# Score blocks of 32 keys by 96 queries on 64x32 array tiles, with an int32 band mask, in a fused sliding-window attention and expert-attention kernel

## The chip, the cores and the metric

The kernel runs on one core of one Trainium2 chip. The core has five engines that run from queues of their own and wait for each other with semaphores: TensorE (PE in the profile, its weight loads are PEld), VectorE (DVE), ScalarE (ACT), GpSimd (POOL) and SyncE (SP), which issues most of the DMAs. The metric is the device time in microseconds of one execution; the lower the better. The runs of the kernel before took 235.07, 235.68 and 236.68 us, with a median of 235.68 us.

## The reference, cut to what matters

Two stages follow each other. The first is attention in a sliding window of 32 keys to either side, over 8 batches, 8 heads, 576 positions and 64 dimensions. The second takes the result as `x` (8 x 576 x 512) and runs four experts, each a causal attention with one head of 64 dimensions, of which two are chosen per token by a gate.

```python
# stage 1
scores = scale * np.matmul(q, k.transpose(0, 1, 3, 2))
mask = np.abs(pos[:, None] - pos[None, :]) <= 32
scores = np.where(mask, scores, -1e9)
attn = softmax(scores); attn_out = attn @ v          # per head
# stage 2
logits = x @ w_gate                                   # two best of four experts
for e in range(E):
    q = x @ wq[e]; k = x @ wk[e]; v = x @ wv[e]
    ye = causal_softmax(scale * q @ k.T) @ v @ wo[e]
    out += weight_of(e) * ye
```

Only the band of the first stage's scores matters: key `k` counts for queries `k - 32` to `k + 32`. A block of 32 keys that starts at `32 n` is therefore needed for the 96 queries from `32 n - 32` to `32 n + 64`, and a block of 64 keys for 128 queries.

## The kernel before, in words

All of the work is cut into small steps, and `ORDER` (lines 29 to 101) lists them by hand in one long order: a name, digits for batch, head group and part, a letter for the engine, and after `@` the PSUM banks. The loop at the end (lines 745 to 755) issues the steps in this order, so each engine's queue holds its own share of the list. SP's loads are tied to their place: a load waits for the matmul that was issued last before it (`load`, line 196). Work of several batches is interleaved: the second stage of one batch stands between the first-stage steps of the next.

The steps that this document speaks of:

- `lq`, `lk`, `lv` load q, k and v. `tq` and `tk` (DVE, a transpose by blocks of 32, line 318) bring q and k to `T` with the head dimension on partitions; 32 partitions hold half a head. For batches 2 to 7 `qc` and `kc` (copies on POOL or ACT) and `mv` (four DMAs from SP, line 367) rearrange `T` so that a whole head of 64 dimensions stands on 64 partitions; this is called paired. Batch 0 gets the paired form by matmuls (`hq`, `hk`), batch 1 stays unpaired and uses matmuls with 32 rows.
- `sc` (line 389) computes the scores of one half of the queries (288 of 576) for four heads of a group, transposed: keys on the partitions, queries along the bank. Four banks hold four heads. The partition of a key is its number modulo 128, so a bank holds in each column the keys of a band about that query. A block has 64 keys, and its place `par` (partitions 0 to 63 or 64 to 127) alternates; `BLK` gives its range of queries and `SEQ` the order of the blocks. In the paired form each block is one matmul per head; the two values of `p` are the two row groups of 64 partitions, `dh` picks one of the two heads there. All 288 columns of all 128 partitions get written. Batch 0 (`NBS`) adds the mask as a matmul of -1e30 (`NB`, built by `s_nb` on DVE at line 222 from `MASKP`).
- `ex` (line 418) takes the exponential of two banks on ACT, into the float32 tile `A`.
- `mk` (line 421) multiplies `A` in place by the 0/1 band mask on POOL, for batches 1 to 7: 56 instructions of 128 x 576 elements. The mask `MASKP` is built once by POOL (`s_mask`, line 204).
- `av` multiplies `A` with the values on PE (float32, in tiles of 128x64 and 128x32); `un` normalises on DVE; `xt`, `xf`, `xb` transpose the result and cast it for the second stage.
- `pp`, `pe`, `pv`, `ve`, `ps`, `xe`, `se`, `po`, `oe`, `pt`, `ot`, `py`, `ye`, `st` and the gate steps `ga` to `gu` are the second stage, in bf16 but for the gate. `ps` with chunk 3 and some others use 64x64 array tiles.

Most matmuls and transposes are issued through the helpers at lines 191 and 194, so the profile gives these lines, and the tiles tell the steps apart: `PS<-T` is `sc`, `PS<-V,A` is `av`, `PS<-QKE` is `ps`, `PS<-XTF,WG` is `ga`, `PS<-ident,XN` is `xt`. A float32 matmul appears as two matmul rows with a weight load each.

## Time and profile before

| | before |
|---|---|
| median of three runs | 235.68 us |
| profiled execution: its time / its span | 234.73 us / 233.0 us |
| PE busy | 216.2 us (93%) |
| DVE / ACT / POOL busy | 168.2 / 161.3 / 158.9 us |
| matmul rows of `sc` (`PS<-T`) | 1440, 41.1 us busy |
| band mask on POOL (line 423) | 56 x 1412 ns, 78.2 us |

The profile is of one execution. Busy time of an engine is the time in which at least one of its instructions ran; matmuls are pipelined and their ends are modelled, so a row's length is not its cost, and the distance between the starts of successive rows says more. "Idle before, and what released it" is the time that an engine stood still just before an instruction of a group. The granted clock is a share of TensorE's full speed; its mean over the span is 0.98.

### The profile page before, as it was taken

To read this page: it belongs to the slowest core of one execution; us is meant where nothing else is said; L and a number is where in the kernel's file an instruction comes from. 1 tells how busy PE (TensorE), PEld (TensorE's weight loads), DVE (VectorE), ACT (ScalarE), POOL (GpSimd) and SP (SyncE) were. 2 spreads that over 40 slices of the span, in tenths; PEclk is the share of its full clock that TensorE was granted. 3 is DMA by queue.
4 is the path that set the end of the run, shared out by engine and by line. 5 is a ranking of instruction groups with operands and counts; after the bars stand their busy time and mean duration, and the time that the engine had idled before them with its cause. 6 is when DMAs were issued, how large, how long until landed. Compare 5 with 4: busy or idle time off the path is not lost. (4 is left out here: it accounts for less than half of the span.)

```text
span 233.0 us, 11640 instructions
## 1 busy us (share of the span) xinstructions
PE 216.2 (93%) x5089; PEld 174.4 (75%) x5100; DVE 168.2 (72%) x328; ACT 161.3 (69%) x246; POOL 158.9 (68%) x205
## 2 busy tenths in 40 slices
PE   7959959999999999999999999999999999999981
PEld 3948846778787887879778888877887778786750
DVE  1744896596899797986898699867864766748760
ACT  2225257888679868778898787758837858678742
POOL 7007037698699997996988998999909982831400
PEclk9999986999999999999999999999999999999998
DMA  6977995889899998988988789946526205051355
GB/s 217 288 202 205 267 348 128 230 222 254 234 259 242 252 303 263 278 190 230 331 252 198 190 254 286 272 150 153 122 53 183 93 3 199 9 207 59 147 205 203
DMA packets 57107, 47.69 MB, mean 205 GB/s; under 512 B 40416, under 2 KB 42976, under 8 KB 57056
## 3 DMA queue, kind: packets, MB, share of 16 engines
q1 hardware_dynamic: 56480, 45.76, 69.3%
q10 hardware_dynamic: 576, 1.18, 1.4%
q8 instruction: 40, 0.66, 1.3%
q14 instruction: 11, 0.09, 0.1%
HBM read 30.42 MB, written 9.44 MB: 171 GB/s over the span
## 5 line engine op out<-in xcount | busy, mean ns | idle before, releaser
L423 POOL TENSOR_TENSOR A<-A,MASKP 128x576 f32<-128x576 f32 x56 | 78.2, 1412 | 5.7 <-ACT A L419 5.4
L619 ACT ACTIVATE ATE<-PS 128x1024 bf16<-128x1024 f32 x48 | 47.9, 1026 | 6.0 <-PE PS L191 5.8
L624 POOL TENSOR_SCALAR_AFFINE_SELECT ATE<-ATE 128x256 bf16<-128x256 bf16 (+1 forms) x80 | 29.0, 382 | 28.7 <-ACT ATE L619 20.3
L419 ACT ACTIVATE A<-PS 128x576 f32<-128x576 f32 x64 | 38.0, 652 | 14.2 <-PE PS L191 12.9
L191 PE MATMUL PS<-T 64*64 64x128 f32 (+7 forms) x1440 | 41.1, 275 | 2.6 <-issue 2.2
L191 PE MATMUL PS<-V,A 128*64 128x65 f32 (+1 forms) x1280 | 39.4, 222 | 0.6 <-DMA V<-in_v_dram 0.5
L191 PEld LDWEIGHTS PS<-V,A 128*64 128x64 f32 (+1 forms) x1280 | 36.4, 132 | 4.6 <-issue 1.5
L191 PEld LDWEIGHTS PS<-T 64*64 64x64 f32 (+1 forms) x1440 | 34.8, 139 | 5.9 <-issue 2.8
L318 DVE STREAM_TRANSPOSE T<-qn 128x1152 f32<-128x1152 f32 x14 | 32.7, 2333 | 7.2 <-PE PS L191 5.2
L318 DVE STREAM_TRANSPOSE T<-kn 128x1152 f32<-128x1152 f32 x14 | 32.7, 2334 | 6.3 <-PE PS L191 5.6
L185 POOL COPY V<-V 64x2048 f32<-64x2048 f32 (+1 forms) x13 | 22.0, 1696 | 14.1 <-DMA V<-in_v_dram 13.8
L452 DVE TENSOR_TENSOR XN<-PS,RC 128x512 f32<-128x512 f32 x32 | 22.1, 691 | 1.2
L185 POOL CAST XTB<-XTF 128x1024 bf16<-128x1024 f32 (+1 forms) x24 | 15.4, 663 | 8.0 <-ACT XTF L183 5.0
L183 ACT COPY Y<-PS 128x1024 f32<-128x1024 f32 (+1 forms) x19 | 15.8, 849 | 5.2 <-PE PS L191 3.1
L183 ACT CAST QKE<-PS 128x576 bf16<-128x576 f32 x22 | 13.9, 644 | 7.5 <-PE PS L191 7.4
L191 PE MATMUL PS<-WO,OTT 128*128 128x512 bf16 (+2 forms) x99 | 17.9, 347 | 1.2 <-ACT OTT L183 0.5
L191 PE MATMUL PS<-WV,XTB 128*128 128x256 bf16 (+1 forms) x192 | 18.6, 256 | 0.0
L183 ACT COPY XTF<-PS 128x1024 f32<-128x1024 f32 (+1 forms) x16 | 13.6, 855 | 7.3 <-PE PS L194 5.6
L191 PE MATMUL PS<-XTB,WQ 128*64 128x288 bf16 (+1 forms) x176 | 18.6, 289 | 0.0
L191 PE MATMUL PS<-QKE 64*64 64x64 bf16 (+9 forms) x256 | 18.3, 279 | 0.1
L191 PEld LDWEIGHTS <-ATE 128*128 128x128 bf16 x480 | 16.3, 97 | 2.7 <-issue 0.9
L191 PE MATMUL PS<-XTB,WK 128*64 128x288 bf16 (+1 forms) x176 | 18.2, 286 | 0.0
(85 smaller groups left out, 301.5 us busy)
## 6 DMA issues: line engine op xcount, KB each, us to landing
V<-in_v_dram SPq DMA_DIRECT2D x32, 256.0 KB, 4.7
out_dram<-Y SPq DMA_DIRECT2D x16, 512.0 KB, 4.6
kn<-in_k_dram SPq DMA_DIRECT2D x28, 288.0 KB, 5.0
qn<-in_q_dram SPq DMA_DIRECT2D x28, 288.0 KB, 5.3
T<-T SPq DMA_DIRECT2D x48, 144.0 KB, 4.1
V<-in_v_dram SPq DMA_DIRECT2D x8, 128.0 KB, 5.1
out_dram<-Y SPq DMA_DIRECT2D x16, 64.0 KB, 3.0
qn<-in_q_dram SPq DMA_DIRECT2D x2, 320.0 KB, 4.4
```

The source lines that it names most:

```text
L183: nc.scalar.copy(o, i)
L185: eng(c).tensor_copy(o, i)
L191: last_pe[0] = nc.tensor.matmul(*a, **kw)
L318: nc.vector.transpose(T.rearrange("q h (p o) -> q h o p", o=18)[:, :, o0:o1, :], x[:, :, o0:o1, :])
L419: nc.scalar.activation(AT[(2 * b + g) % NAT_][half][p], two(b0)[:, :, 0:HS], EXP, scale=scale_att)
L423: eng(c).tensor_tensor(out=ap, in0=ap, in1=MASK[:, None, HS * half:HS * half + HS].to_broadcast([128, 2, HS]), op=MULT)
L452: nc.vector.tensor_tensor(out=XN[T // 2][:, T % 2, :].rearrange("p (t h d) -> p h t d", t=4, h=8), in0=u[:, :, 0:64].rearrange("p h (d t) ...
L619: nc.scalar.activation(chunk(A, ch), two(b0), EXP, scale=scale_moe)
L624: nc.gpsimd.affine_select(ap, ap, pattern=[[0, n], [1, w]], compare_op=IS_GE, fill=0.0, base=0, channel_multiplier=-1)
```

## The change

The scores of batches 2 to 7 are cut into blocks of 32 keys. The partition group of block `n` is `32 * (n % 4)`, as before a key's number modulo 128, and the block gets only the queries of its band within the half, at most 96. `blocks32` lists the blocks of a half for both values of `dh` in an order that gives the next block to the column group with the fewest columns so far. Each matmul names its place in the array (64 rows by 32 columns). Of each 128 columns a group of 32 partitions now gets 96 written; the other 32 keep what earlier steps left in the bank. `ex` reads the same range as before. The mask tile becomes int32, and `mk` multiplies the bits of `A` as integers by 0 or 1. Batches 0 and 1 keep their score matmuls; batch 1 uses the new `mk`. `ORDER`, banks and all other steps are unchanged.

```diff
-    MASKP = sb.tile([128, SP_], F32, name="MASKP")
+    MASKP = sb.tile([128, SP_], I32, name="MASKP")
...
-        nc.gpsimd.memset(MASKP, 1.0)
+        nc.gpsimd.memset(MASKP, 1)
...
-        nc.gpsimd.memset(MASKP[64:128, 0:64], 0.0)
-        nc.gpsimd.memset(MASKP[64:128, 576:640], 0.0)
+        nc.gpsimd.memset(MASKP[64:128, 0:64], 0)
+        nc.gpsimd.memset(MASKP[64:128, 576:640], 0)
...
+    def blocks32(half):
+        c0 = HS * half
+        todo = [[], [], [], []]
+        for n in range(S // 32):
+            lo, hi = max(c0, 32 * n - 32), min(c0 + HS, 32 * n + 64)
+            if lo < hi:
+                todo[n % 4] += [(n, lo, hi, 0), (n, lo, hi, 1)]
+        at, seq = [0] * 4, []
+        while any(todo):
+            col = min((i for i in range(4) if todo[i]), key=lambda i: at[i])
+            seq.append(todo[col].pop(0))
+            at[col] += seq[-1][2] - seq[-1][1]
+        return seq
+
+    SEQ32 = [blocks32(0), blocks32(1)]
+
     def sc(c, b, g, half, b0, b1):
         bank = (b0, b0 + 1, b1, b1 + 1)
         c0 = HS * half
 
         add = b in NBS
+        if PAIRED[g] and not add:
+            for n, lo, hi, dh in SEQ32[half]:
+                o = 32 * (n % 4)
+                for p in range(2):
+                    r = slice(64 * p, 64 * p + 64)
+                    mm(PS[o:o + 32, bank[2 * p + dh], lo - c0:hi - c0],
+                       QKT[g][r, 2 * dh, 1, 32 * n:32 * n + 32], QKT[g][r, 2 * dh, 0, lo:hi],
+                       start=True, stop=True, skip_group_check=True, tile_position=(64 * p, o))
+            return
...
     def mk(c, b, g, half, p):
-        ap = AT[(2 * b + g) % NAT_][half][p]
+        ap = AT[(2 * b + g) % NAT_][half][p][:, :, :].bitcast(I32)
         eng(c).tensor_tensor(out=ap, in0=ap,
                              in1=MASK[:, None, HS * half:HS * half + HS].to_broadcast([128, 2, HS]), op=MULT)
```

More of the change, by code (lines that the diff above doesn't have):

```diff
@@ L10 @@
 BF16 = mybir.dt.bfloat16
+I32 = mybir.dt.int32
 EXP = mybir.ActivationFunctionType.Exp
```

## The prediction

> **What bounds the kernel now.** I read the page first (busy shares), then the waits, then busy time by stretch, then the order of instructions in time on TensorE and GpSimd.

> ```profile
> span 233.0 us, 11640 instructions
> PE 216.2 (93%) x5089; PEld 174.4 (75%) x5100; DVE 168.2 (72%) x328; ACT 161.3 (69%) x246; POOL 158.9 (68%) x205
> ```
> ```profile
> ACT A L419 <- PE PS L191: 12.9, 15, 2.7
> DVE T L318 <- PE PS L191: 10.8, 6, 2.9
> PE PS L191 <- DMA V<-in_v_dram: 0.5, 1, 0.5
> ```
> ```profile
> 50.00:70.00 20.00, 19.31 (x476) 16.30 (x474) 16.82 (x27) 15.64 (x24) 17.06 (x24) 1.00 0.90 243
> 70.00:90.00 20.00, 19.70 (x515) 16.33 (x510) 16.77 (x30) 16.57 (x25) 18.38 (x23) 1.00 0.93 262
> 90.00:110.00 20.00, 19.43 (x507) 16.07 (x504) 16.61 (x28) 16.00 (x28) 17.67 (x19) 1.00 0.92 247
> 110.00:130.00 20.00, 19.89 (x485) 16.54 (x484) 16.88 (x27) 16.37 (x27) 18.11 (x20) 1.00 0.89 246
> 130.00:150.00 20.00, 20.00 (x456) 16.54 (x449) 17.70 (x32) 16.89 (x26) 19.19 (x22) 1.00 0.89 248
> ```

> From 50 us on TensorE (PE) is busy 19.3 to 20.0 of every 20 us. A busy PE is not proof, because its ends are modelled; the waits decide it. The other engines wait for PE over and over (ACT 12.9 us before the exponentials, DVE 10.8 us before the transposes), and PE's own waits are tenths of a microsecond, the longest of this kind 0.5 us for a V load. So PE sets the pace. It does not do so by much: the columns of the last view are PE, weight loads, DVE, ACT, POOL, then clock, DMA share and GB/s, and POOL (GpSimd) adds up to 90.4 of the 100 us from 50 to 150, the DMA engines are 0.89 to 0.93 busy. What PE gains can be spent only until one of these is full.

> **The change, part 1: the score matmuls.** It touches `sc` of batches 2 to 7: 6 batches x 2 head groups x 2 halves = 24 steps. Each float32 matmul stands as two in the trace. Rows from TensorE in order of time (start, length, shape of the array tile, count):

> ```profile
> 12.21 1.21 PE L191 MATMUL PS<-T 64*64 64x64 f32 x40
> 13.21 0.46 PE L191 MATMUL PS<-OTT,ident_bf 64*64 64x288 bf16 x8
> ...
> 41.31 1.36 PE L191 MATMUL PS<-T 32*64 32x64 f32 x80
> 42.60 1.29 PE L191 MATMUL PS<-XTF,WG 128*32 128x160 f32 x32
> ...
> 93.23 2.29 PE L191 MATMUL PS<-T 64*64 64x64 f32 x80
> 95.45 1.29 PE L191 MATMUL PS<-XTF,WG 128*32 128x160 f32 x32
> ```
> ```profile
> 118.25 1.29 PE L191 MATMUL PS<-XTF,WG 128*32 128x160 f32 x32
> 119.48 0.70 PE L191 MATMUL PS<-QKE 64*128 64x320 bf16 x8
> ...
> 173.56 1.28 PE L191 MATMUL PS<-T 64*64 64x64 f32 x40
> 174.78 1.55 PE L194 MATMUL PS<-ident,XN 64*64 64x64 f32 x40
> ```

> Now: a step has 20 matmuls (40 rows) on four 64x64 tiles. Its widths per parity are 96+128+64 and 160+128, 288 columns, for two head halves `dh`: 576 columns per tile. The step at 12.21 is followed by matmuls of its own tile shape after 1.00 us; the one at 173.56 by another kind after 1.22. So 1.00 us is the streaming, 1.74 ns a column, and 0.22 us the emptying of the array that a change of shape costs. Two steps in a row (93.23 to 95.45) take 2.22 = 2 x 1.00 + 0.22, which fits.

> After: blocks of 32 keys on eight 64x32 tiles (2 row groups, 4 column groups). A half has ten blocks, with `dh` and the row group 40 matmuls (80 rows): twice the instructions. Columns: 64, seven of 96, 64 and 32. The busiest column group holds 64+96+64 = 224 (or 96+96+32), with two `dh` 448 columns, in place of 576.

> Does a column cost the same there? No row shows 64x32 tiles. Two neighbours bound it. Four column tiles of 128x32 (118.25): 16 matmuls of 160 columns, 640 per tile, in 1.23 us; less the 0.22 that is 1.58 ns a column. Eight tiles of 32x64 (41.31 to 42.60): 576 per tile in 1.29, less 0.22, 1.86 ns. So 448 columns take 0.71 to 0.83 us. I take 0.80, toward the row with eight tiles: 0.20 us less per step, **24 x 0.20 = 4.8 us** (4.1 to 7.0). With twice the matmuls on fewer columns this hangs on the instruction rate: 80 rows in 0.80 us is one in 10 ns. The 32x64 step runs one in 13 ns (1.07/80) while bound by its columns, so 10 is just beyond what is shown.

> [...]

> Lost covers: where a score step stood beside another 64x64 step, the array did not have to empty; with 64x32 it must.

> ```profile
> 113.16 2.52 PE L191 MATMUL PS<-T 64*64 64x64 f32 x80
> 115.43 0.47 PE L191 MATMUL PS<-QKE 64*64 64x448 bf16 x8
> ...
> 160.43 0.43 PE L191 MATMUL PS<-QKE 64*64 64x512 bf16 x4
> ```

> Reading down TensorE's order I count six such borders from 50.98 to 160.43 (two of them around 113.16), each worth 0 to 0.22 us. I take 0.15: **0.9 us back**. Net on PE 3.9 us (2.8 to 7.0).

> **Part 2: the int32 mask.** The blocks cover the band exactly, 96 of every 128 query columns for a group of 32 keys, so the rest of the bank holds what earlier steps left. The exponential reads it (same shape as before) and the multiply by an integer 0 must clear it, whatever its bits. The 56 multiplies on POOL go from float32 to int32, same bytes, same two inputs.

> ```profile
> L423 POOL TENSOR_TENSOR A<-A,MASKP 128x576 f32<-128x576 f32 x56 | 78.2, 1412 | 5.7 <-ACT A L419 5.4
> L185 POOL COPY T<-T 128x576 f32<-128x576 f32 x14 | 9.2, 661 | 2.4 <-DVE T L318 1.9
> L222 DVE TENSOR_SCALAR OTT<-MASKP 64x640 bf16<-64x640 f32 x4 | 1.9, 486 | 0.0
> ```

> No row has POOL at an integer operation. From below: it moves as many elements as the copy with one input, 661 ns; from above I allow twice the float32 multiply, 2.8 us. The nearest row is the float32 multiply itself, 1412 ns, and I take that: **0 us**. [...]

> The mask itself is built once by POOL at the start; after it POOL stands idle 12.77 us until 18.28, so int32 fills there cost nothing. `s_nb` on DVE reads it four times at 486 ns from 7.39, with 0.54 us free behind it; were each twice as long, the first scores would start 1.4 us later. I take 0.

> ```profile
> 18.28 3.42 POOL L185 COPY V<-V 64x1536 f32<-64x1536 f32 x2 [12.77 <-DMA V<-in_v_dram]
> ```
> ```profile
> 7.39 1.98 DVE L222 TENSOR_SCALAR OTT<-MASKP 64x640 bf16<-64x640 f32 x4
> 9.91 0.82 DVE L185 COPY T<-PS 128x640 f32<-128x640 f32 x1 [0.54 <-PE PS L191]
> ```

> **What of the 3.9 us reaches the end.** Order and waits on ACT, DVE, POOL and SP stay as they are; PE alone gets shorter, and loads follow it, since SP's loads are tied to places in PE's list. Where a score step is late because its moved quarters (`mv`, SP) land late, a shorter step gains little:

> ```profile
> 148.40 2.54 SPq L367 DMA_DIRECT2D T<-T  x4
> ```
> ```profile
> 151.22 1.96 PE L191 MATMUL PS<-T 64*64 64x64 f32 x64
> 153.42 0.76 PE L191 MATMUL PS<-T 64*64 64x160 f32 x16 [0.24 <-issue]
> ```

> The fourth of these transfers is issued just before 151, and the pair from 151.22 needs 2.9 us in place of 2.2. That pair's 0.4 us I write off, and 0.1 for smaller cases of the kind. Is POOL in time? Its latest products for the value matmuls:

> ```profile
> 174.88 1.96 POOL L624 TENSOR_SCALAR_AFFINE_SELECT ATE<-ATE 128x256 bf16<-128x256 bf16 x5 [5.43 <-ACT ATE L619]
> ...
> 187.40 4.14 POOL L423 TENSOR_TENSOR A<-A,MASKP 128x576 f32<-128x576 f32 x3
> ```
> ```profile
> 190.02 1.15 PE L191 MATMUL PS<-V,A 128*64 128x65 f32 x32
> ```

> The first of the three multiplies ends near 188.8 and its user starts at 190.02: 1.2 us of slack, with PE then over 3 us ahead of today. But POOL stood idle 5.4 us at 174.88 waiting for ACT, which waits for PE, so it moves forward too. The sum is 4.8 - 0.9 - 0.5 = **3.4 us**. The profiled execution took 234.73 us (span 233.0 and 1.7 around it), which gives a span of 229.6 and 231.3 us. The median of the runs is 235.68, 0.95 above that execution, so the forecast for a median is **232.3 us**, 1.4% faster.

> **Rivals.**
> 1. *Absorbed (no change, 234 to 237).* PE's gain turns into PE's waits. For it: from 50 to 150 POOL must fit 90.4 us and the DMA engines about 90 into 97, with the order fixed for the old lengths. Against it: the waits point from everyone to PE, and POOL's own idle time is mostly for ACT behind PE. If two thirds go, 1.1 us stay: 234.6.
> 2. *The int32 multiply is slower (slower than before).* Place: POOL, 40 multiplies from 50 to 150.

> ```profile
> 50.00:70.00 20.00, 7.93 (x6) 1.00 0.90 243
> 70.00:90.00 20.00, 11.78 (x9) 1.00 0.93 262
> 90.00:110.00 20.00, 10.81 (x9) 1.00 0.92 247
> 110.00:130.00 20.00, 9.05 (x7) 1.00 0.89 246
> 130.00:150.00 20.00, 11.43 (x9) 1.00 0.89 248
> ```

>    With d more for each, POOL holds 90.4 + 40 d. That passes PE's 96.6 at d = 0.155 us (11%), and the old 100 at 0.24 us (17%); from there the kernel is slower. At half as much again (0.71) it is 118.8: 19 us more, 254. At twice, 56 us more in this stretch less the 9.6 free, 47: 282 and over. [...]
> 3. *The matmuls do not pack (slower).* If each of the 80 rows keeps the spacing of the 64x64 pair, 2.22/80 = 27.8 ns, a pair takes 4.4 us and 12 pairs cost 26.6 us more: 262. [...] Against it: the 13 ns at 41.31.

> **Chances and range.** Forecast 0.52; absorbed 0.20; slow integer multiply 0.22, of which 0.01 so little that nothing shows; no packing 0.06. So faster by over 1% 0.52, within 1% (about what a measurement of this kernel can tell from no change) 0.21, slower 0.27. The forecast's own range is 229.3 to 233.3: net 2.8 to 7.0 us on PE, less the 0.5. The range of eight in ten goes to 246, a multiply about a third slower (40 x 0.47 = 18.8, less 9.6 free, is 9 us over), and leaves out the dearer multiplies (0.13), the matmuls that don't pack and a little below.

> **What would show it.** PE's rows `PS<-T` become 64*32, about 2400 in place of 1440; two steps in a row last 1.8 us (1.6 to 1.9) in place of 2.2: right for part 1; 4.4 would be rival 3. The group L423, then int32, should read near 1412 ns; above 1570 POOL binds, with waits of PE on POOL and no more idle time of POOL on ACT. If both are as I say and the span stays, the waits of PE on DMA, DVE or ACT must have grown, and rival 1 holds. What would make me wrong beyond these: a clock granted at less than 1.00 after 50 us, or the exponential taking longer on what the banks hold outside the band.

## The result

The changed kernel is slower. Its runs took 263.25, 263.48, 265.22 and 271.65 us, median 264.35, and a fifth 267.16, beside 235.07 to 237.18, median 236.18, for the kernel before on the same chip. The profiled execution is the one of 271.65 us, a slow one, which the ratio leaves out: the ratio of the means of the others to before is 1.121, with a 95% interval of 1.110 to 1.132. The forecast was 232.3 us and its range ended at 246.0. A second profile of the same kernel (268.51 us, below under `after_again`) stops at every instruction at which this one stops for long.

First the page of the changed kernel: span and busy times, the granted clock in 40 slices, the queue that brings instructions, the shares of the chain that ended last, and two of the costliest groups. New lines shift the numbers: the helper at 191 is now 192, and the instructions of `ex` and `mk` have the lines 447 and 452.

```profile
span 269.9 us, 13560 instructions
...
PE 228.1 (84%) x6049; PEld 179.8 (67%) x6060; DVE 168.9 (63%) x328; ACT 161.8 (60%) x246; POOL 159.0 (59%) x205
...
PEclk9988998999996799799959997999799899999998
...
q8 instruction: 47, 0.77, 1.2%
...
PE 72%; issue 12%; ACT 5%; POOL 3%; DVE 3%; DMA 3%; SPq 1%; ACTq 0%; DVEq 0%
...
L452 POOL TENSOR_TENSOR A<-A,MASKP 128x576 int32<-128x576 int32 x56 | 78.1, 1409 | 8.3 <-ACT A L447 8.1
...
L192 PE MATMUL PS<-T 64*32 64x96 f32 (+9 forms) x2400 | 39.8, 249 | 20.3 <-issue 19.7
```

DVE, ACT and POOL have the busy times of before, within 0.7 us. PE's rose by 11.9 us, in an execution with far more half clock than before (5 in the row PEclk; the experiments come back to it), but its share fell from 93% to 84%: it stands idle for 41.8 us of the span, in place of 16.8. The chain says what kind of idle time this is: 12% of the span, some 32 us, is "issue", time in which PE waited for nothing that the profile shows. The last group carries 19.7 us of that kind ahead of the score matmuls. The int32 multiply takes 1409 ns, as the float32 one did (1412).

The waits of the changed kernel (engine, line, waited for: total us, times, longest):

```profile
POOL ATE L653 <- ACT ATE L648: 37.6, 11, 5.4
ACT A L447 <- PE PS L192: 28.8, 20, 3.7
PEld PS L192 <- issue: 28.5, 29, 4.0
PE PS L192 <- issue: 26.4, 14, 3.9
```

And of the kernel before, the row of the same kind, which the prediction left out:

```profile
PE PS L191 <- issue: 2.2, 2, 1.9
```

From 2.2 us in 2 waits to 26.4 us in 14. ACT and POOL still wait for PE, directly or by way of ACT, for longer than before. By stretch, in the order of columns used in the prediction:

```profile
50.00:70.00 20.00, 16.52 (x544) 13.29 (x547) 14.39 (x28) 12.46 (x19) 14.80 (x23) 1.00 0.80 212
70.00:90.00 20.00, 16.13 (x430) 13.24 (x420) 13.02 (x15) 14.14 (x23) 15.17 (x18) 0.84 0.79 210
90.00:110.00 20.00, 15.15 (x565) 12.37 (x564) 13.34 (x21) 11.97 (x18) 14.59 (x15) 0.99 0.64 197
110.00:130.00 20.00, 18.23 (x503) 15.04 (x502) 13.26 (x25) 12.76 (x21) 12.15 (x14) 0.91 0.73 199
130.00:150.00 20.00, 16.15 (x410) 11.83 (x404) 12.47 (x21) 11.84 (x20) 13.01 (x14) 0.83 0.56 161
```

PE is busy 82.2 of these 100 us (98.3 before), and the mean clock of four stretches is below 1.00 (0.83 to 0.99). The DMA engines have room now: 0.56 to 0.80 busy, where they were at 0.89 to 0.93.

Where PE stands still is seen in its order in time (start, length, row group, idle before in brackets):

```profile
51.86 2.29 PE L192 MATMUL PS<-T 64*32 64x64 f32 x160
54.08 0.41 PE L192 MATMUL PS<-QKE 64*64 64x320 bf16 x8
54.51 1.27 PE L192 MATMUL PS<-V,A 128*64 128x65 f32 x36
58.12 1.04 PE L192 MATMUL PS<-V,A 128*64 128x65 f32 x28 [2.33 <-issue]
...
78.70 2.06 PE L192 MATMUL PS<-T 64*32 64x32 f32 x160 [0.21 <-ACT VE L184]
80.68 0.62 PE L192 MATMUL PS<-WO,OTT 128*64 128x512 bf16 x4
84.97 1.06 PE L192 MATMUL PS<-WO,OTT 128*64 128x512 bf16 x4 [3.66 <-issue]
...
104.77 2.10 PE L192 MATMUL PS<-T 64*32 64x32 f32 x151
110.77 0.32 PE L192 MATMUL PS<-T 64*32 64x64 f32 x9 [3.90 <-issue]
```

Two things stand here. A pair of score steps that nothing disturbs takes 1.98 us (78.70 to 80.68): shorter than the 2.22 of before, not as short as the 1.80 forecast. And just behind such a pair, or nine rows from the end of one, PE stops for 2 to 4 us in the middle of a row of like matmuls: between the 36th and the 37th of one `av`, between the fourth and the fifth of one `po`, between the 151st and the 152nd row of one score pair. The profile shows no late tile there: the idle time is "issue", and the next matmul belongs to the same step as the last.

Counting PE's instructions (matmuls, weight loads and some 60 waits for semaphores) up to each stop gives the place. A stop is measured here from the start of the last instruction ahead of it to the next start, so it holds the 0.2 to 0.4 us of that last matmul too and is a little longer than the idle time in the rows above. All twelve stops of more than 0.8 us between 40 and 215 us come at the same point of a block of 256:

```
changed kernel: stop at us, its length, instructions recorded before it, (that number + 67) mod 256
 55.6 2.56  2751   2  |  68.6 0.83  3263   2  |  80.9 4.04  4031   2
 98.5 1.85  4798   1  | 106.6 4.12  5309   0  | 125.0 1.20  6077   0
132.4 3.64  6589   0  | 156.0 0.94  7613   0  | 159.2 2.99  7869   0
181.3 1.65  8893   0  | 189.8 2.55  9404 255  | 210.5 2.26 10428 255
```

The 67 is the shift that fits all of them; the count is of records, of which a few can be missing, hence 2 at the start and 255 at the end. The instruction queue's row tells of the same unit: 47 packets with 0.77 MB are 16.4 KB each, and the changed kernel has 12,172 recorded instructions on PE, 47.5 blocks of 256; the kernel before has 40 packets and 10,252 instructions, 40.0 blocks. Such a packet starts after PE enters a block (0.4 to 3.2 us after, from 50 to 215 us of this execution), and what it brings is needed at the end of that block. A changed pair is 160 matmul rows with as many weight loads, 320 instructions in 2 us, more than a whole block. **The theory that was tested: PE used up its instructions faster than blocks of them came in, and stood still until the next block was there.** The rivals were that the new tile shape or the unwritten banks slow PE down, that the int32 multiply does, and that only the data transfers hold the blocks up.

### The profile page after: what moved, and what is told of

Its sections match the earlier page's. It is cut to its first block, busy times and chain, and to the rows that moved or that the text cites. A ratio compares the mean times of both kernels' runs of the same rounds, so it can differ in the third digit from the quotient of the medians.

```text
span 269.9 us, 13560 instructions
## 1 busy us (share of the span) xinstructions
PE 228.1 (84%) x6049; PEld 179.8 (67%) x6060; DVE 168.9 (63%) x328; ACT 161.8 (60%) x246; POOL 159.0 (59%) x205
## 4 chain that ended last, share of the span: by engine, by line
PE 72%; issue 12%; ACT 5%; POOL 3%; DVE 3%; DMA 3%; SPq 1%; ACTq 0%; DVEq 0%
PE PS L192 65%; PE PS L195 5%; POOL A L452 3%; PE PS L239 2%; DMA V<-in_v_dram 2%; DVE T L319 1%; ACT XTF L184 1%; DMA T<-T 1%; SPq L198 1%; ACT A L447 1%; ACT ATE L648 1%; ACT V L184 1%; DVE XTF L186 0%; POOL XTB L186 0%; ACT VE L184 0%
## 5 line engine op out<-in xcount | busy, mean ns | idle before, releaser
L452 POOL TENSOR_TENSOR A<-A,MASKP 128x576 int32<-128x576 int32 x56 | 78.1, 1409 | 8.3 <-ACT A L447 8.1
L447 ACT ACTIVATE A<-PS 128x576 f32<-128x576 f32 x64 | 38.2, 651 | 32.2 <-PE PS L192 28.8
L192 PE MATMUL PS<-T 64*32 64x96 f32 (+9 forms) x2400 | 39.8, 249 | 20.3 <-issue 19.7
L192 PEld LDWEIGHTS PS<-T 64*32 64x32 f32 (+2 forms) x2400 | 33.8, 113 | 25.6 <-issue 22.4
L192 PE MATMUL PS<-V,A 128*64 128x65 f32 (+1 forms) x1280 | 40.7, 227 | 2.5 <-issue 2.3
L192 PEld LDWEIGHTS PS<-V,A 128*64 128x64 f32 (+1 forms) x1280 | 37.8, 136 | 6.9 <-issue 4.6
L186 POOL COPY V<-V 64x2048 f32<-64x2048 f32 (+1 forms) x13 | 22.0, 1693 | 13.3 <-DMA V<-in_v_dram 12.9
L192 PE MATMUL PS<-WO,OTT 128*128 128x512 bf16 (+2 forms) x99 | 18.8, 363 | 4.7 <-issue 3.7
L192 PE MATMUL PS<-XTB,WQ 128*64 128x288 bf16 (+1 forms) x176 | 20.2, 304 | 1.8 <-POOL A L452 1.0
L192 PE MATMUL PS<-WV,XTB 128*128 128x256 bf16 (+1 forms) x192 | 20.6, 272 | 0.7 <-issue 0.7
L192 PE MATMUL PS<-XTB,WK 128*64 128x288 bf16 (+1 forms) x176 | 20.9, 307 | 0.0
L192 PEld LDWEIGHTS <-ATE 128*128 128x128 bf16 x480 | 17.6, 102 | 2.6 <-issue 1.1
L192 PE MATMUL PS<-VE,ATE 128*128 128x65 bf16 x480 | 19.0, 200 | 0.0
```

The lines of the kernel that those rows point to most:

```text
L186: eng(c).tensor_copy(o, i)
L192: last_pe[0] = nc.tensor.matmul(*a, **kw)
L447: nc.scalar.activation(AT[(2 * b + g) % NAT_][half][p], two(b0)[:, :, 0:HS], EXP, scale=scale_att)
L452: eng(c).tensor_tensor(out=ap, in0=ap, in1=MASK[:, None, HS * half:HS * half + HS].to_broadcast([128, 2, HS]), op=MULT)
```

## The experiments

Each was compared with the kernel before on the same chip. "Stops" are those of over 0.45 us at the end of a block of 256 instructions that begin between 50 and 215 us of the span, measured as above; the kernel before has two, with 1.0 us.

### The int32 mask alone

```diff
-    MASKP = sb.tile([128, SP_], F32, name="MASKP")
+    MASKP = sb.tile([128, SP_], I32, name="MASKP")
...
-        ap = AT[(2 * b + g) % NAT_][half][p]
+        ap = AT[(2 * b + g) % NAT_][half][p][:, :, :].bitcast(I32)
```

> The kernel before with the int32 mask and the int32 multiply alone; scores as before. Theory A (TensorE's instructions arrive in blocks of 256, and 160 rows per score step use them up faster than the next block comes): 234 to 238 us, the multiply at 1.41 us. Theory B (64x32 tiles stall inside the array): the same. Theory C (the integer multiply or its data cost the time): 250 us or more.

Measured: 236.32 us beside 235.97, a ratio of 1.003 (0.998 to 1.008): no difference. The group of the multiply, on its page:

```profile
L424 POOL TENSOR_TENSOR A<-A,MASKP 128x576 int32<-128x576 int32 x56 | 78.3, 1414 | 5.8 <-ACT A L420 5.4
```

1414 ns for int32, 1412 for float32. The mask is out of it; the score blocks make the loss.

### The new tiles with few instructions

The changed kernel with each 64x32 tile given one matmul of 288 columns per head half: 32 rows per step on the same eight tiles, in place of 80.

```diff
-                todo[n % 4] += [(n, lo, hi, 0), (n, lo, hi, 1)]
+                todo[n % 4].append((n, lo, hi))
+        for i in range(4):
+            n = todo[i][0][0]
+            todo[i] = [(n, c0, c0 + HS, 0), (n, c0, c0 + HS, 1)]
```

> The kernel after, with the score steps of batches 2 to 7 still on eight 64x32 tiles, but one matmul per tile and head half, 288 columns wide: 16 matmuls (32 rows) per step in place of 40 (80). It leaves out the right scores (each group of 32 partitions uses the keys of its first block alone). Columns per tile: 576, as on 64x64 tiles before. Theory A: no idle time of TensorE on issue of a microsecond or more from 50 us on, two steps in a row in 2.1 to 2.3 us, 233 to 238 us in all. Theory B: steps of 2.5 us and more, 250 us or more.

Measured: 233.86 us beside 235.97, a ratio of 0.995 (0.991 to 0.9996). A pair in time, and PE's wait:

```profile
72.65 2.18 PE L192 MATMUL PS<-T 64*32 64x288 f32 x64 [0.21 <-ACT VE L184]
74.76 1.05 PE L192 MATMUL PS<-WO,OTT 128*64 128x512 bf16 x8
```
```profile
PE PS L192 <- issue: 1.6, 3, 0.8
```

The long stops are gone (1.6 us in all), with the tile shape and the int32 multiply still there. So the shape isn't what costs. This kernel also writes every column of the banks; that unwritten parts don't cost either is shown by the next one, which stops with all columns written. The pair is 2.11 us for 576 columns per tile and step; less the 0.12 to 0.22 that the rows show where another tile shape follows (`e7_half_dose` and the kernel before), that is 1.64 to 1.73 ns a column, within the 1.58 to 1.86 that the prediction took from its two neighbours.

### More instructions on the old tiles

The kernel before, each score matmul of batches 2 to 7 cut in two by columns: 80 rows per step as in the changed kernel, 64x64 tiles, float32 mask.

```diff
+                mid = (lo + hi) // 2
+                for lo_, hi_ in (((lo, hi),) if add else ((lo, mid), (mid, hi))):
-                for p in range(2):
+                    for p in range(2):
```

> The kernel before (float32 mask, 64x64 tiles), each score matmul of batches 2 to 7 cut in two halves by columns: 40 matmuls (80 rows) per step, the same columns. Theory A: TensorE idle on issue for 15 to 30 us, in pieces of 1 to 4 us, 255 to 268 us in all. Theory B: 235 to 240 us.

Measured: 263.8 us (261.78 and 265.82) beside 235.97. Its order in time and its wait:

```profile
78.11 3.02 PE L191 MATMUL PS<-T 64*64 64x32 f32 x160 [0.21 <-ACT VE L183]
81.06 0.62 PE L191 MATMUL PS<-WO,OTT 128*64 128x512 bf16 x4
84.71 1.06 PE L191 MATMUL PS<-WO,OTT 128*64 128x512 bf16 x4 [3.03 <-issue]
```
```profile
PE PS L191 <- issue: 17.9, 16, 3.1
```

The stop behind the pair at 78 is there again, after the same matmul of the same step, without new tiles, without int32 and without unwritten columns. The number of instructions alone makes the stops: 19.7 us of them, and the nine over 0.8 us between 40 and 215 us all stand at one point of a block of 256 again (instructions 2753, 3009, 4033, 4801, 5313, 6081, 6593, 7873 and 9409; remainder 4 with the shift used above). The pair itself takes 2.95 us in place of 2.22, with twice the rows for the same columns on the same four tiles (18.4 ns a row). The 24 steps, eleven pairs and two alone, count as 12 pairs: 12 x 0.73 = 8.8 us. With 18.7 us more of stops the sum is 27.5, and the span rose by 27.1 (260.1 against 233.0).

### The same columns in three pieces

The kernel with 288 columns per tile, each matmul cut into three of 96: 96 rows per step, more than the changed kernel has.

```diff
-            todo[i] = [(n, c0, c0 + HS, 0), (n, c0, c0 + HS, 1)]
+            todo[i] = [(n, c0 + 96 * j, c0 + 96 * j + 96, dh) for j in range(3) for dh in range(2)]
```

> As the wide blocks, but each 288 columns cut in three of 96: 48 matmuls (96 rows) per step on 64x32 tiles, still 576 columns per tile, scores again not the right ones. Theory A: 384 instructions per pair of steps, TensorE idle on issue 25 to 45 us, 262 to 282 us in all. On the side, in a step without such a stop: if a row cannot be issued faster than about 11 ns, the 96 rows last 1.05 to 1.1 us from first to last start; if the columns bind as in the wide blocks (0.80 us from first to last start for 288-wide matmuls), 0.9 to 1.0.

Measured: 271.86 us (268.72 and 275.0) beside 236.43.

```profile
79.97 2.46 PE L192 MATMUL PS<-T 64*32 64x96 f32 x192 [0.21 <-ACT VE L184]
82.36 1.05 PE L192 MATMUL PS<-WO,OTT 128*64 128x512 bf16 x8
```
```profile
PE PS L192 <- issue: 24.8, 16, 3.6
```

From 233.86 to 271.86 us by cutting alone: same tiles, same columns, same data. (The wait is just under the 25 us expected; the time lies within.) The undisturbed pair also tells the rate: 192 rows in 2.39 us and 160 in 1.98 are both 12.4 ns a row, and within one step from the first row to the last it is 1.119 us for 96 rows and 0.91 for 80, 11.7 and 11.4 ns. On these tiles it is the rows that set the step, not the columns.

### Half the dose

The changed kernel with the new blocks in the first half of the queries alone: 240 instructions per pair in place of 320 (160 before).

```diff
-        if PAIRED[g] and not add:
+        if PAIRED[g] and not add and half == 0:
```

> The kernel after with blocks of 32 keys in the score steps of the first half of the queries alone; the second half on 64x64 tiles as before: 240 instructions per pair of steps. Theory A with a threshold at blocks of 256: fewer and shorter stops, 240 to 250 us. Proportional to the number of changed steps: about 250.

Measured: 242.05 us (240.18 and 243.93) beside 236.43.

```profile
PE PS L192 <- issue: 9.3, 11, 2.5
```

Half of the added instructions bring 10 stops with 10.4 us, and the two runs are 3.8 and 7.5 us above the median of before: an eighth and a quarter of the 28 us, not a half. The loss depends on how fast one block is used against how fast the next comes, not on the sum of instructions.

### Lighter transfers

Two kernels ask why a block comes late. The first is the changed kernel without the loads of q, k and v from batch 3 on (the lines below stand in the two functions that load); the second has them in `mv` too and leaves out its transfers. Both compute on old data.

```diff
+        if b >= 3:
+            return
```

> The kernel after without the loads of q, k and v from batch 3 on (the tiles keep older data). Theory A, if the blocks of instructions wait behind data transfers: idle on issue falls from 26 us to 10 to 16, 243 to 254 us in all. Theory A with a delay that does not depend on the load: 258 to 266 us. Theory B: 258 to 266 us.

> The changed kernel without the loads of q, k and v and without the transfers of mv from batch 3 on, so that from there the DMA engines carry the blocks of instructions and the outputs alone. If the blocks are late because they queue behind data, a block is usable within 3 us of being asked for, idle on issue falls below 10 us and the time to 238 to 246. If most of the delay is fixed (a block's own transfer of 1 us and what follows it), it stays near 4 us, idle on issue 13 to 16 us, 246 to 250 us as with the loads alone left out.

Measured: 248.64 us beside 235.97 without the loads, 246.55 (244.57 and 248.52) beside 234.41 without the moves as well. The stretch from 50 to 150 us and PE's wait, first of the one and then of the other:

```profile
50.00:150.00 100.00, 87.76 (x2878) 71.79 (x2875) 74.06 (x117) 71.97 (x112) 81.33 (x96) 0.98 0.31 77
```
```profile
PE PS L192 <- issue: 15.5, 14, 2.0
```
```profile
50.00:150.00 100.00, 90.22 (x2924) 74.72 (x2922) 77.03 (x122) 74.91 (x116) 82.55 (x97) 0.98 0.17 48
```
```profile
PE PS L192 <- issue: 12.7, 12, 1.9
```

The DMA engines' share falls from 0.71 to 0.31 and 0.17, the rate from 196 to 77 and 48 GB/s. The stops get shorter and don't go: 17.1 and 14.1 us are left of 29.4 to 29.8. So other transfers explain two fifths to a half of what PE waits, and the rest stays with nearly empty engines. For the second kernel the expectation of a mostly fixed delay is the nearer one: 12.7 us of wait, not under 10, and a block usable after 3.6 us, not within 3 (table below).

### Batch 1 in the paired form

The kernel before has a stop of this kind too, in the one pair of steps that already had 160 matmul rows, batch 1's scores on 32x64 tiles:

```profile
30.90 0.82 PE L191 MATMUL PS<-T 32*64 32x64 f32 x40
33.66 3.60 PE L191 MATMUL PS<-T 32*64 32x96 f32 x120 [1.94 <-issue]
```

The test rearranged batch 1 too, which halves the instructions of those steps.

```diff
-    ... ex0010@0 hk010@6
+    ... ex0010@0 kc10:a hk010@6
-    ... ex0110@4 av04@4
+    ... ex0110@4 qc10:a mv10 av04@4
-    ... ex1011@2 wm1@7
+    ... ex1011@2 kc11:a qc11:a mv11 wm1@7
```

> The kernel before with batch 1 paired too (kc, qc and mv for both groups of batch 1): its four score steps take 80 instructions each in place of 160. Theory A: the stop on issue of about 2 us near 32 us goes; 232 to 235 us if nothing else holds that stretch. If TensorE waits for the weights and the first x of the second stage there anyway: 235 to 237 us.

A miss: 243.84 us beside 236.43, a ratio of 1.033 (1.023 to 1.042).

```profile
36.29 5.46 PE L191 MATMUL PS<-T 64*64 64x64 f32 x80 [3.36 <-DMA T<-T]
```

The stop for instructions is gone from this place and a wait of 3.36 us for the moved quarters is there instead, with a longer step behind it. It says nothing against the theory and is no way to a faster kernel as it was placed.

### The changed kernel again

> The changed kernel itself once more, for a profile beside the others on one chip: 260 to 267 us, TensorE idle on issue 22 to 28 us.

Measured: 268.51 and 269.72 us beside 234.41, a ratio of 1.149 (1.137 to 1.161). The time is 2 us above what was expected; PE's wait lies within.

```profile
PE PS L192 <- issue: 27.5, 18, 4.4
```

It stops at the same instructions (2751, 3263, 4031, 4798, 5309, 6077, 6589, 7613, 7869, 8893, 9404 and 10428, and two more at 2495 and 6333). What comes behind a stop in the clock can be read around the one that ends at 84.6 us (columns as before):

```profile
81.00:84.40 3.40, 0.19 (x2) 0.00 (x0) 2.03 (x1) 1.09 (x3) 3.40 (x7) 1.00 1.09 258
84.40:87.80 3.40, 3.22 (x48) 2.51 (x47) 0.28 (x2) 1.19 (x2) 1.19 (x2) 0.50 0.76 180
87.80:91.20 3.40, 3.40 (x121) 2.94 (x113) 3.35 (x4) 3.19 (x7) 0.95 (x3) 1.00 0.39 145
```

PE does next to nothing for 3.4 us, then gets half the clock for 3.4 us (48 matmuls), then the full one (121). Without the last 4 us of each span, this execution has 23.9 us at half clock, the first profile of the changed kernel 34.1, the kernel before 6.8.

### All runs by one sum

```
                      blocks  packet     stops     usable after entry  fastest use
                      (n)     ends after n, us     us, median (range)  of a block
before                30      2.5        2,  1.0   4.4 (4.1-4.7)       3.6
int32 mask alone      30      2.1        2,  1.7   5.3 (5.0-5.7)       3.6
batch 1 paired        29      2.1        1,  0.9   7.6                 3.9
new tiles, few instr. 28      2.4        2,  1.8   4.9 (4.9-5.0)       3.9
half dose             32      2.6       10, 10.4   4.6 (3.8-5.3)       2.6
old tiles, cut        33      2.6       13, 19.7   4.2 (3.3-7.6)       2.2
changed               32      2.6       14, 29.8   4.7 (3.4-5.9)       1.5
changed, again        32      2.5       14, 29.4   4.5 (3.6-6.2)       1.5
three by 96           35      2.4       18, 31.5   4.2 (3.3-5.8)       1.5
changed, no loads     35      2.3       12, 17.1   3.8 (2.6-4.5)       1.5
 and no moves         36      2.1        9, 14.1   3.6 (2.7-5.2)       1.5
```

Counted from the traces, 50 to 215 us: the blocks; the median time from entering a block (its first instruction starts) to the end of the packet that brings the next; the stops; the time from entering a block until PE went on with the next, where it had stopped; and the shortest time in which a block was used, without the stop behind it. Packets and blocks can be paired one to one, and in all 97 stops PE went on 1.1 to 1.8 us after the recorded end of the packet that brought the block it went on with. This ties the end of a stop to the packet, and not only its place to the count. In the median a block is there 3.6 to 5.3 us after the one ahead of it is entered (7.6 at the one stop with batch 1 paired). The kernel before never uses one in less than 3.6 us and hardly stops; the kernels that use one in 1.5 to 2.6 us stop nine to eighteen times.

| span less that of before (233.0) | measured | stops, less 1.0 | 12 x change of a pair | half of the added time at half clock | sum |
|---|---|---|---|---|---|
| changed | 36.9 | 28.8 | -2.9 | 13.7 | 39.6 |
| changed, again | 33.8 | 28.3 | -2.9 | 8.5 | 33.9 |
| old tiles, cut | 27.1 | 18.7 | 8.8 | 0 | 27.5 |
| three by 96 | 34.0 | 30.5 | 2.0 | 3.4 | 35.9 |
| half dose | 9.2 | 9.4 | 0.8 | -1.7 | 8.5 |

The clock's term is an upper bound, since not all of that time hung on PE. With it the stops, the pairs and the clock account for the spans to within 3 us.

## Why the prediction was wrong

**Part 1, the gain per step: mis-sized.** "24 x 0.20 = 4.8 us" came from columns: 448 at 1.58 to 1.86 ns. The column's price was right (1.64 to 1.73 in the run with few instructions), but it isn't what ends the step. The prediction said that "this hangs on the instruction rate: 80 rows in 0.80 us is one in 10 ns", and took 10 as just beyond what was shown. The tiles give one row in 11.4 to 11.7 ns, so the step takes 0.91 us and a pair 1.98: 0.12 us less per step, 2.9 us in all, where no stop falls into it.

**Part 1, what is missing: the supply of instructions.** "Order and waits on ACT, DVE, POOL and SP stay as they are; PE alone gets shorter" holds no term for it. The phrase "twice the instructions" was there, but they were counted as rows through the array and not as bytes that must be brought in (16.4 KB for 256 of them). This step failed, and it is the whole loss: 28 to 29 us more of stops than before, and the clock lost behind them. No rival held it either; the 0.27 that was given to "slower" stood on the multiply and on the packing, and neither of them came. The trace of before held what was needed: the waits "PE PS L191 <- issue: 2.2, 2, 1.9", and the one pair of steps with 160 rows, batch 1's, which stood still for 1.94 us after its first 40. The prediction read the waits from 50 us on and took the spacing on 32x64 tiles from a single batch-1 step (41.31); the stop in the pair, at 31.7 us, was not looked at. Blocks of 256 were there 4.1 to 4.7 us after the one ahead was entered where PE had to wait for them; 320 instructions in 1.8 us use one in 1.4. From these, an estimate made in hindsight is a stop of 2 to 3 us at most of the 12 pairs, 24 to 36 us in all.

**The 0.5 us for late quarters: misread.** The row at 153.42 in the kernel before, 0.24 us of idle time "<-issue", was put down to a transfer of `mv`. It stands at instruction 7357, the end of a block of 256, and PE went on 1.4 us after an instruction packet had ended, as in the other stops; the changed kernel stops 0.49 us at the same instruction. The trace shows no late tile there.

**The borders.** Behind the 64x32 step the next kind of tile starts 0.12 us after the last row (0.91 to 1.03, in the half-dose run), so six of these would be 0.7, for 0.9 forecast. That the array empties in this time is the prediction's reading; the rows show the time alone. The count of six was short: PE's order before has 64x64 matmuls just ahead of the pairs at 93.23, 113.16, 128.31, 133.52 and 151.22 and just behind those at 50.98, 113.16 and 158.23, eight borders, which would be 1.0. They were not measured by themselves.

**Part 2, the mask: right.** 1409 to 1419 ns in every run with it, and alone it makes no difference. The second rival (slow integer multiply) falls. The exponential, named as a danger, takes 651 ns, and 652 before.

**Rival 1 (absorbed)** falls: the gain was not turned into waits for other engines; those wait for PE still. **Rival 3 (no packing)** gave 262 us, near the result, for a reason that the rows refute: its pair was to last 4.4 us, and lasts 1.98 where nothing stops it. **The clock below 1.00 after 50 us**, named as what would make the forecast wrong, did come, and it goes with the stops: the kernel before, the one with the int32 mask alone and the one with few instructions on the new tiles have 1.00 from 50 to 150 us, and every stretch of half clock in the changed kernel between 50 and 215 us begins in a stop or within 1.4 us behind it. Not every long stop brought one (2.56 us at 55.6 did not).

**Still open** is why a block takes so long to be there. From entering a block to the start of the packet it is 0.9 to 1.6 us in the median and up to 3.9 in the changed kernel; the packet takes 1.0 to 1.2; and PE goes on 1.3 to 1.5 us after the packet's recorded end, as the median of each run's stops. Taking most data transfers away took a fifth to a quarter off the median time until a block was usable (4.5 and 4.7 to 3.6 us). What the rest consists of, the traces don't show.

## What to carry to other kernels

Count instructions per microsecond on TensorE, weight loads included (a float32 matmul stands as four in these traces, two rows with a weight load each), before cutting matmuls finer: here 256 instructions had to last about 4 to 5 us, and a stretch that used them in 1.5 us stood still for the difference. Idle time put down to "issue" in the middle of a row of like matmuls, at distances that are multiples of 256 instructions, was the sign of this stop here (all twelve of over 0.8 us in the first profile stand at such distances); a dose test (the same columns in more or fewer pieces) showed it in one run, 263.8 us beside 235.97 for the old tiles, cut. Fewer columns on finer tiles paid less here than their number promised: on eight 64x32 tiles the rows set the step, at one in 11.4 to 11.7 ns, and 448 columns a tile took 0.91 us in place of the 0.80 forecast.
